# When a planner gives back a buffer of gate-output sums, and which addition the last quad's third product stands behind

## The chip, the cores and the metric

The kernel runs on one core of one Trainium2 chip. The metric is the device time of one execution in microseconds (us); lower is better. Before the change it is 394.08 us, the median of three runs (394.03 to 394.35).

## The reference

Multi-head attention feeds a two-layer network with a SiLU between the layers. Shapes: batch 8, 12 heads, 448 tokens, head size 64; so 3584 tokens of width 768, and an inner width of 2048.

```python
scores = scale * np.matmul(q, k.transpose(0, 1, 3, 2))
attn = softmax(scores)                       # over the keys
x = np.matmul(attn, v).transpose(0, 2, 1, 3).reshape(3584, 768)
h = x @ w_in                                 # 768 -> 2048
g = h * (1.0 / (1.0 + np.exp(-h)))           # SiLU
out = g @ w_out                              # 2048 -> 768, float32
```

## The kernel before, in words

**Units of attention.** A unit is one batch with four of its heads (the first batch's units are cut in two pieces of tokens). For each unit TensorE makes scores into PSUM (tiles `s`, line 345), ScalarE takes the exponential (`E`, line 382), VectorE adds two or three of the exponentials for the row sums (`T`, line 393), TensorE makes the sums and then the two products with V (tiles `a`, lines 408 and 424; "part 1" and "part 2" of a unit), and VectorE normalizes each part into `xT` (`norm`, line 479). Keys and queries come in by DMA (`rk`, `rq`) and are transposed by VectorE (`KT`, line 314; `rq`, line 332). Units mostly go in pairs; the pair spoken of here is 11 and 12, followed by units 13, 14 and so on.

**First layer.** `ffn1` (tiles `h`) multiplies `xT` with `w_in`; ScalarE's tanh (line 517) and VectorE's `gate` (line 552) make the gate outputs `G` (some of them stand in `X`). The last two batches are done as a pair of tokens' blocks with tiles `f`, lines 626 to 681.

**Second layer.** The tokens are cut into 28 tiles of 128, and two tiles make a quad: quads 0 to 13. Quad 0 is done plainly (tiles `o`). Each other quad is a two by two by two block product done with seven products of eight matmuls instead of eight products (Strassen's way, in Winograd's form). The products are called 1, 5, 6, 2, 7, 3, 4, in the order in which they are queued, and lie in PSUM tiles `p`. Products 1, 6, 7 and 4 all accumulate into the bank of product 1, the long bank, and between them each state of it is read out: after 1 and 6 and 4 by a ScalarE copy (`take_copy`, line 767), after 7 by a VectorE addition (`take_sum`, line 773). Product 3 accumulates into the bank of product 5, product 2 has its own. An addition or a copy writes an output tile `ost`, and `store` sends it out.

**The gate-output sums.** Products 5, 6 and 3 take a sum of gate outputs as their stationary operand. VectorE makes it in two halves (`combine_g`, line 696, 128x512 each): sum 5 from `G` alone (`S<-G`), sum 6 from sum 5 (`S<-S,G`, or `S<-S,X`), sum 3 from sum 6 (`S<-G,S` or `S<-X,S`). Product 7 takes a difference that is written over `G` (`G<-G`). The sums live in three buffers, tag `S`, `NSG` = 3. So sum 5 is read by product 5 and by the two halves of sum 6; sum 6 by product 6 and by the two halves of sum 3; sum 3 by product 3 alone.

**What sets the order.** The order on every engine is drawn before the program is built, by a planner (`Order`) that walks through time with a cost for each step: when an engine is free in it, it picks the next step whose inputs are ready. The steps are then issued in that order, and each engine works through its own list in order. Buffers that rotate are counted by rings: a sum is planned only when `sg_ring` has a free place,

```python
while todo and (todo[0] == 7 or sg_ring.can(1, od.now)):
    m = todo.pop(0)
    if m != 7:
        sg_ring.take()
```

and a place is given back at the end of the product that reads the sum (`op.then = sg_ring.give`, line 1199). The ring is the planner's count only. Which of the three buffers a sum gets, and the semaphores that hold its writer back until all readers of the former contents are done, come from the tile pool when the program is built.

**Waits between products.** In `queue(m)` of a quad, `first` names the read-outs that product m stands behind: those in `hard` must be done in the planner's time, the others need only have been placed already (`(took.get(x), 9.0)`). For m = 3 `first` is (5, 6, 7), of which 5 is hard. TensorE's array is used in three ways: by rows of 32 (scores), by columns of 32 (attention products, 32 small matmuls where a whole one takes 8), and whole. `times` with `strips` makes a layer's product by columns where the planner's state is "cols", so that the array isn't switched; the lists show such a product as x32 or x24 and a whole one as x8 or x6.

Of the kernel before, what the change touches and what calls it, by code (L numbers as in the profile page):

```python
# [25 lines left out]
def mm(n):  # L26
    return n / 2400.0 + 0.0026


def act(n):  # L30
    return n * 0.00087 + 0.13
# [138 lines left out]
def kernel(  # L170
# [11 lines left out]
    B, NH, S, D = q.shape  # L182
# [14 lines left out]
    NT = 2 * S // 128  # L197
# [14 lines left out]
    NE, NX3, NT_ = 9, 6, 2  # L212
    NXT = 3 * NX3
    NSG, NOST = 3, 7
    attn_scale = 1.0 / (D**0.5)

    const = ctx.enter_context(tc.tile_pool(name="const", bufs=1))
# [467 lines left out]
    def combine_g(qd, m, f0, f1):  # L685
        a, b = 2 * qd, 2 * qd + 1
        if m != 7 and (qd, m) not in S_t:
            S_t[(qd, m)] = sb.tile([128, HF, 128], FP16, name=f"S_{qd}_{m}", tag="S", bufs=NSG)
        x, y, op = {
            5: (rows(b, 0), rows(b, 1), ALU.add),  # L690
            6: (S_t.get((qd, 5)), rows(a, 0), ALU.subtract),
            7: (rows(a, 0), rows(b, 0), ALU.subtract),
            3: (rows(a, 1), S_t.get((qd, 6)), ALU.subtract),
        }[m]
        dst = rows(b, 0) if m == 7 else S_t[(qd, m)]
        nc.vector.tensor_tensor(out=dst[:, f0:f1], in0=x[:, f0:f1], in1=y[:, f0:f1], op=op)  # L696
# [3 lines left out]
    def product(qd, m, strips):  # L700
        w = {1: rows(2 * qd, 0), 2: rows(2 * qd, 1), 4: rows(2 * qd + 1, 1), 7: rows(2 * qd + 1, 0)}
        w = w[m] if m in w else S_t[(qd, m)]
        if BANK[m] == m:
            pr_t[(qd, m)] = ps.tile([128, 512], FP32, name=f"p_{qd}_{m}", tag="m", bufs=4)
        for f in range(HF):
            times(
                pr_t[(qd, BANK[m])][:, 0:OH],
                w[:, f, :],
                W_[m][:, f, :],
                f == 0 and BANK[m] == m,  # L710
                f == HF - 1,
                strips,
            )
# [174 lines left out]
    sg_ring, ost_ring = Ring(NSG), Ring(NOST)  # L888
# [240 lines left out]
    def batches(qd):  # L1129
        return {  # L1130
            (128 * t + c) // S for t in (2 * qd, 2 * qd + 1) for c in (0, 127)
        }

    def plan_sums():

        if not quads:
            return
        qd, todo = quads[0]
        if len(todo) == 4:
            gates = {}  # L1140
            for b in batches(qd):
                for f in range(NFF):
                    if len(g_op.get((b, f), ())) < (len(PIECES) if b == 0 else 1):
                        return
                    gates.setdefault(f, []).extend(g_op[(b, f)])
            gates_of[qd] = gates
        gates = gates_of[qd]
# [4 lines that stand above are left out]
            sg_op[(qd, m)] = []  # L1152
            for f0 in (0, 4):
                deps = [x for f in range(f0, f0 + 4) for x in gates[f] + gates[f + HF]]
                if m != 5:
                    deps += sg_op[(qd, {6: 5, 7: 5, 3: 6}[m])]
                sg_op[(qd, m)].append(
                    od.add(
                        Op(
                            "DVE",  # L1160
                            0.34,
                            lambda m=m, f0=f0: combine_g(qd, m, f0, f0 + 4),
                            deps,
                            0,
                        )
                    )
                )
        if not todo:
            quads.pop(0)

    def queue_quad(qd):
        quads.append((qd, [5, 6, 7, 3]))
        took = {}
        home = far_ring if qd in FAR else ost_ring

        def read(m, deps):
            def then(at):
                if m in (2, 3, 4):
                    m_ring.give(at)
                if m in (2, 3, 4, 7):  # L1180
                    home.give(at + STORE)

            fn, eng = (take_copy, "ACT") if m in OUT else (take_sum, "DVE")
            busy = act(OH) if eng == "ACT" else OH / 960.0 + 0.13
            bias = -2 if eng == "ACT" else -4
            took[m] = od.add(Op(eng, busy, lambda: fn(qd, m), deps, bias, then=then))

        def queue(m):
            first = {6: (1,), 2: (1,), 7: (6, 5), 3: (5, 6, 7), 4: (7,)}.get(m, ())

            def run():
                strips = od.mode == "cols" and bool(qk_seq or av_seq)
                op = Op("PE", HF * mm(OH), lambda: product(qd, m, strips), tail=PE_OUT)
                if BANK[m] == m:
                    m_ring.take()
                for ring, need in rings:
                    ring.take(need)
                if m in (5, 6, 3):
                    op.then = sg_ring.give
                od.on_pe(op, "cols" if strips else "full")  # L1200
                pr_op[(qd, m)] = op
                read(m, [op] + [took[x] for x in {2: (1,), 7: (5,), 3: (6,)}.get(m, ())])

            def deps():
                made = list(w_op.get(m, [None]))
                hard = {6: (1,), 7: (6,), 3: (5,), 4: (7,)}.get(m, ())
                made += [took.get(x) if x in hard else (took.get(x), 9.0) for x in first]
                if m in (1, 2, 4):
                    t = 2 * qd + m // 4
                    i = int(m != 1)  # L1210
                    for b in {(128 * t + c) // S for c in (0, 127)}:
                        for f in range(HF):
                            x = g_op.get((b, f + HF * i), [None])
                            made += [(y, f * mm(OH)) for y in x]
                    return made + ld_wout
                x = sg_op.get((qd, m), [None, None])
                return made + [x[0], (x[1], 4 * mm(OH))]

            rings = ((home, 1),) if m in OUT else ()
            moe.append((deps, 1 if BANK[m] == m else 0, run, rings))  # L1220


        for m in (1, 5, 6, 2, 7, 3, 4):
            queue(m)
# [238 lines left out]
    while True:  # L1463
        plan_turns(qk_seq[0][0][0] + 3 if qk_seq else NU)
        plan_adds()
        plan_pair()
        plan_silu()
        plan_sums()
        soon = od.step()
        if od.free["PE"] <= od.now:  # L1470
# [78 lines left out]
```

## Time and profile before

| what | value |
|---|---|
| median of three runs | 394.08 us (394.03 to 394.35) |
| the profiled execution's own time | 394.92 us |
| its span, first to last instruction | 393.1 us |
| granted TensorE clock | 1.000 |
| TensorE matmul busy | 384.6 us (98%) |
| VectorE busy | 274.4 us (70%) |
| ScalarE busy | 253.9 us (65%) |
| GpSimd busy | 89.0 us (23%) |

The profile names engines PE (TensorE matmul), PEld (its weight loads), DVE (VectorE), ACT (ScalarE), POOL (GpSimd) and SP (SyncE). A row of the timeline has the start in us from the first instruction, the time that it covers, the engine, the line of the kernel, the operation, the tile written and those read, and how many instructions of that kind follow each other; in square brackets stands how long the engine sat idle before it, and what ended that. The end of a matmul is modelled and lies after the point where the next can start, so the time that TensorE takes for a group is read from its start to the start of the next group. Buffer numbers are left out of the tiles' names: `S` is any of the sums, `xT` any of the normalized tiles.

### The profile page before, as it was taken

Reading aid. Unit: us, or ns where it says so; the run is one execution under the profiler, and the core shown is the slowest. Engines: PE = TensorE matmul, PEld = TensorE weight load, DVE = VectorE, ACT = ScalarE, POOL = GpSimd, SP = SyncE. Lnnn points to the kernel's source line nnn. Section 1 sums busy time; section 2 is a strip of 40 time slices with the busy share of each in tenths; the row PEclk is TensorE's granted clock in tenths of the full one; section 3 lists DMA queues with packets and bytes.
Section 4 is the critical chain, followed back from the end, with each engine's and each line's share of the span. In section 5 each row is a group of like instructions: output and inputs, shape, how many; then the busy total and the mean of one; then the engine's idle time right before and its main releaser. Section 6 shows DMA issues by size and latency. Waiting matters only on the chain.

```text
span 393.1 us, 10622 instructions
## 1 busy us (share of the span) xinstructions
PE 384.6 (98%) x4345; PEld 206.3 (52%) x4345; DVE 274.4 (70%) x570; ACT 253.9 (65%) x399; POOL 89.0 (23%) x173
## 2 busy tenths in 40 slices
PE   7999999999998999999999999999999999999995
PEld 6657774444454444545445444544445555556663
DVE  2466676999977787868678758665969984447441
ACT  4977885797765779766683766567793338882220
POOL 7533365515006252400643005000000000000000
PEclk9999999999999999999999999999999999999999
DMA  8999999929039482905767229102100131001333
GB/s 120 196 202 210 158 147 195 193 43 138 4 55 144 107 117 37 133 21 106 125 92 89 56 64 158 24 0 52 33 2 2 37 96 30 2 1 43 91 93 99
DMA packets 35361, 34.52 MB, mean 88 GB/s; under 512 B 11376, under 2 KB 33776, under 8 KB 35312
## 3 DMA queue, kind: packets, MB, share of 16 engines
q0 software_dynamic: 24784, 22.82, 39.7%
q1 hardware_dynamic: 9952, 10.33, 9.8%
q8 instruction: 34, 0.56, 0.6%
q10 hardware_dynamic: 576, 0.69, 0.5%
q14 instruction: 15, 0.12, 0.1%
HBM read 45.61 MB, written 11.01 MB: 144 GB/s over the span
## 4 chain that ended last, share of the span: by engine, by line
PE 95%; DVE 1%; DMA 1%; ACT 1%; issue 1%; DVEq 0%; POOLq 0%
PE p L491 30%; PE h L491 29%; PE s L345 12%; PE a L408 11%; PE f L491 8%; PE o L491 3%; PE a L424 2%; DMA rk<-in_k_dram 1%; PE z L1458 1%; ACT E L382 1%; DVE KT L314 0%; DVE S L696 0%; DVE rq L332 0%; DVE xT L479 0%; ACT ost L767 0%
## 5 line engine op out<-in xcount | busy, mean ns | idle before, releaser
L382 ACT ACTIVATE E<-s 128x896 f16<-128x896 f32 (+1 forms) x172 | 149.9, 915 | 38.6 <-PE s L345 37.1
L491 PE MATMUL h<-xT,w_in_t 128*32 128x448 f16 (+2 forms) x1086 | 117.1, 336 | 0.0
L491 PEld LDWEIGHTS <-w_in_t 128*128 128x128 f16 (+1 forms) x1158 | 71.1, 97 | 56.4 <-issue 11.5
L517 ACT ACTIVATE th<-h 128x448 f16<-128x448 f32 (+1 forms) x112 | 54.2, 494 | 36.7 <-PE h L491 31.9
L552 DVE SCALAR_TENSOR_TENSOR G<-th,h 128x448 f16<-128x448 f16 (+2 forms) x112 | 55.7, 509 | 23.4 <-ACT th L517 21.8
L767 ACT COPY ost<-p 128x384 f32<-128x384 f32 x52 | 24.9, 480 | 55.2 <-PE p L491 53.6
L491 PEld LDWEIGHTS <-G 128*128 128x128 f16 (+1 forms) x580 | 43.3, 98 | 32.7 <-issue 4.9
L345 PE MATMUL s<-rq,KT 32*128 32x448 f16 (+4 forms) x768 | 50.9, 337 | 1.0 <-DVE rq L332 0.5
L279 POOL DMA_DIRECT2D V<-in_v_dram x88 | 48.3, 558 | 13.3 <-DMA w_out_t<-in_moe_w_out_dram 6.0
L491 PE MATMUL p<-w_out_t,G 128*128 128x384 f16 (+1 forms) x328 | 49.5, 326 | 0.0
L408 PE MATMUL a<-E,V 128*32 128x448 f16 (+2 forms) x864 | 42.5, 333 | 1.3 <-DVE xT L479 1.0
L491 PEld LDWEIGHTS <-S 128*128 128x128 f16 (+1 forms) x384 | 29.8, 98 | 23.1 <-issue 2.7
L260 POOL DMA_DIRECT2D rq<-in_q_dram x27 | 15.1, 558 | 104.6 <-PE s L345 79.2
L491 PE MATMUL p<-D,S 128*128 128x384 f16 (+1 forms) x232 | 37.1, 326 | 0.0
L479 DVE SCALAR_TENSOR_TENSOR xT<-a,rdn 128x448 f16<-128x448 f32 (+1 forms) x54 | 30.4, 568 | 6.4 <-PE a L408 4.5
L345 PEld LDWEIGHTS <-KT 32*128 32x128 f16 (+2 forms) x864 | 17.5, 98 | 29.4 <-issue 27.6
L773 DVE TENSOR_TENSOR ost<-p,ost 128x384 f32<-128x384 f32 x39 | 21.6, 553 | 16.1 <-PE p L491 12.6
L408 PEld LDWEIGHTS <-V 128*32 128x32 f16 (+1 forms) x864 | 20.8, 96 | 20.1 <-issue 8.8
L393 DVE TENSOR_TENSOR T<-E,E 128x1792 f16<-128x1792 f16 x20 | 21.6, 1081 | 8.0 <-ACT E L382 8.0
L393 DVE TENSOR_TENSOR T<-T,E 128x1792 f16<-128x1792 f16 x20 | 21.6, 1082 | 5.7 <-ACT E L382 5.7
L314 DVE STREAM_TRANSPOSE KT<-rk 128x256 f32<-128x256 f32 (+3 forms) x48 | 16.6, 384 | 6.6 <-DMA rk<-in_k_dram 6.1
L491 PE MATMUL p<-D,G 128*32 128x384 f16 (+1 forms) x176 | 19.1, 326 | 0.4 <-DVE ost L773 0.4
(67 smaller groups left out, 320.4 us busy)
## 6 DMA issues: line engine op xcount, KB each, us to landing
out_dram<-ost SPq DMA_DIRECT2D x194, 48.0 KB, 1.6
rk<-in_k_dram POOLq DMA_DIRECT2D x24, 224.0 KB, 5.6
rq<-in_q_dram POOLq DMA_DIRECT2D x21, 224.0 KB, 5.6
w_in_t<-in_moe_w_in_dram POOLq DMA_DIRECT2D x6, 512.0 KB, 12.7
w_out_t<-in_moe_w_out_dram POOLq DMA_DIRECT2D x4, 768.0 KB, 13.5
V<-in_v_dram POOLq DMA_DIRECT2D x43, 64.0 KB, 3.7
V<-in_v_dram POOLq DMA_DIRECT2D x40, 48.0 KB, 3.8
out_dram<-ost SPq DMA_DIRECT2D x8, 96.0 KB, 2.1
```

The lines of the kernel that those rows point to most:

```text
L279: nc.gpsimd.dma_start(out=VT[b][32 * x : 32 * (x + 1), hs, 0:count, :], in_=v[b, hs].rearrange("h (i g) d -> i h g d", g=TPP)[:, :, first ...
L314: nc.vector.transpose(out=pairs[:, x:y, 0:count], in_=t[:, first : first + count * (y - x)].rearrange("p (x c) i -> p x c i", c=count),)
L345: nc.tensor.matmul(out=pS[p0 : p0 + 32 * (x1 - x0), h % 2, at : at + nq], lhsT=KT[(b, hg)][32 * h : 32 * (h + 1), c, x0:x1, :, e], rhs=QT[ ...
L382: nc.scalar.activation(out=E[(n, w)][0:kr, 2 * y : 2 * y + 2, 0:nk], in_=pS_t[(n, w, y)][0:kr, :, 0:nk], func=AF.Exp, scale=attn_scale,)
L393: nc.vector.tensor_tensor(out=T[n], in0=T[n] if step else E[(n, 0)], in1=E[(n, step + 1)], op=ALU.add,)
L408: nc.tensor.matmul(out=a[32 * h : 32 * (h + 1), 0:nq], lhsT=w, rhs=e[k0:k1, h, at : at + nq], start=start, stop=stop,)
L479: nc.vector.scalar_tensor_tensor(out=x3(b, cc)[:, cc % 3, 32 * g0 : 32 * g1], in0=acc[(n, part)][:, 0:nq], scalar=0.5, in1=rdn_t[n].rearra ...
L491: nc.tensor.matmul(out=out[i : i + cut], lhsT=w[:, i : i + cut], rhs=x, start=start, stop=stop, skip_group_check=True,)
L517: nc.scalar.activation(out=th, in_=h_t[(b, f, t0)][:, 0 : t1 - t0], func=AF.Tanh)
L552: nc.vector.scalar_tensor_tensor(out=dst[:, f, at + lo : at + hi], in0=th_t[(b, f, t0)][:, lo - t0 : hi - t0], scalar=1.0, in1=h_t[(b, f, ...
L767: nc.scalar.copy(out=ost(qd, *OUT[m]), in_=bank(qd, BANK[m]))
L773: nc.vector.tensor_tensor(out=t, in0=bank(qd, BANK[m]), in1=t, op=ALU.add)
```

## The change

The planner's ring now gets a buffer back only when all its readers have been placed: the place of sum 5 at the latest end among product 5 and the two halves of sum 6, that of sum 6 at the latest end among product 6 and the two halves of sum 3, that of sum 3 at the end of product 3. And in quad 13, the last, product 3 no longer needs the addition after product 7 to have been placed ahead of it.

```diff
+    LAST = NT * B // 4 - 1
...
+    sum_reads = {}
+
+    def sum_read(qd, m, at):
+        made = sum_reads.setdefault((qd, m), [])
+        made.append(at)
+        if m and len(made) == (1 if m == 3 else 3):
+            sg_ring.give(max(made))
+
     def plan_sums():
...
                             lambda m=m, f0=f0: combine_g(qd, m, f0, f0 + 4),
                             deps,
                             0,
+                            then=lambda at, m=m: sum_read(qd, {6: 5, 3: 6}.get(m), at),
...
-            first = {6: (1,), 2: (1,), 7: (6, 5), 3: (5, 6, 7), 4: (7,)}.get(m, ())
+            first = {6: (1,), 2: (1,), 7: (6, 5), 3: (5, 6) if qd == LAST else (5, 6, 7), 4: (7,)}.get(m, ())
...
                 if m in (5, 6, 3):
-                    op.then = sg_ring.give
+                    op.then = lambda at: sum_read(qd, m, at)
```

No instruction's work is changed by it, only the order that the planner draws. Where both programs are laid side by side, engine by engine, the lists of GpSimd and SyncE are the same, and ScalarE's order is the same; VectorE's list differs in three places, TensorE's in one:

- Quads 1 and 2, VectorE. Before: the difference for product 7 of quad 2 (two halves), the addition after product 7 of quad 1, sum 3 of quad 2 (two halves), the normalization of unit 11 part 2, transpose of `rq` 14, first `T` of unit 13, the addition after product 3 of quad 1, normalization of unit 12 part 1, transpose of `KT`, second `T` of unit 13, normalization of unit 12 part 2, transpose of `rq` 15. After: the addition after product 7 of quad 1, the difference for product 7 of quad 2, transpose of `rq` 14, first `T` of unit 13, the normalization of unit 11 part 2, sum 3 of quad 2, the addition after product 3 of quad 1, transposes of `KT` and `rq` 15, normalization of unit 12 part 1, second `T` of unit 13, normalization of unit 12 part 2. (A little earlier the second half of sum 6 and half of the difference of quad 1 change places with sum 5 of quad 2.)
- The same place, TensorE. Before: product 3 of quad 1 (columns), scores of unit 13, part 1 of unit 12, product 4 of quad 1 (columns), part 2 of unit 12, scores of unit 14, products 5 and 2 of quad 2 (whole), scores of unit 14. After: product 3 of quad 1 (columns), scores of unit 13, product 4 of quad 1 (whole), part 1 of unit 12, scores of unit 14, part 2 of unit 12, products 5 and 2 of quad 2 (columns), scores of unit 14.
- Quads 3 and 4, VectorE. Before: sum 6 of quad 4, the difference for product 7 of quad 4, sum 3 of quad 3, `KT`, `rq` 19, the addition after product 7 of quad 3. After: sum 3 of quad 3, `KT`, sum 6 of quad 4, the difference for product 7 of quad 4, `rq` 19, the addition after product 7 of quad 3. (The second half of sum 6 of quad 3 also goes ahead of sum 5 of quad 4.)
- Quads 8 and 9, VectorE. The tile `sx` for the last two batches (line 600) goes ahead of sum 6 of quad 9, and the addition after product 7 of quad 8 goes between the two halves of the difference for product 7 of quad 9, ahead of sum 3 of quad 9.

In quad 13 no engine's list differs.

## The prediction

> **What bounds the kernel now.** I read the page first, part 4, the chain that ended last:
>
> ```profile
> PE 95%; DVE 1%; DMA 1%; ACT 1%; issue 1%; DVEq 0%; POOLq 0%
> ```
>
> TensorE's work is nearly the whole chain, so the end moves by what TensorE gains or loses and by little else. The change removes no matmul work; it can only take away or add time in which TensorE stands still. So the second view is TensorE's own waits from 100 us on, ahead of every place where the two orders differ:
>
> ```profile
> engine line waited for: us in total, times, longest us
> PE a L408 <- DVE xT L479: 1.0, 1, 1.0
> PE p L491 <- DVE ost L773: 0.4, 1, 0.4
> ```
>
> These are all: two waits, both for VectorE, in the last three quarters of the span. After them the chain in order of time shows nothing but TensorE's groups, and ends with the last quads' products in one unbroken piece:
>
> ```profile
> 353.75 35.12 PE p L491 x216
> ```
>
> 216 matmuls in 35.12 us is 0.163 us each, which is also what one costs inside a group below. There is no hole in the tail.
>
> **The first wait, quads 1 and 2.** TensorE's rows, then VectorE's and two of ScalarE's, from the timeline:
>
> ```profile
> 117.16 1.47 PE L491 MATMUL p<-w_out_t,S 128*32 128x384 f16 x32
> 118.56 0.58 PE L345 MATMUL s<-rq,KT 32*128 32x448 f16 x8
> 120.13 0.94 PE L408 MATMUL a<-E,V 128*32 128x448 f16 x16 [0.99 <-DVE xT L479]
> 120.88 1.49 PE L491 MATMUL p<-D,G 128*32 128x384 f16 x32
> 122.18 0.94 PE L408 MATMUL a<-E,V 128*32 128x448 f16 x16
> 123.06 0.57 PE L345 MATMUL s<-rq,KT 32*128 32x448 f16 x8
> 123.56 1.47 PE L491 MATMUL p<-D,S 128*128 128x384 f16 x8
> 124.87 1.46 PE L491 MATMUL p<-w_out_t,G 128*128 128x384 f16 x8
> 126.27 0.57 PE L345 MATMUL s<-rq,KT 32*128 32x448 f16 x8
> ```
> ```profile
> 115.19 0.74 DVE L696 TENSOR_TENSOR G<-G 128x512 f16<-128x512 f16 x2
> 115.85 0.55 DVE L773 TENSOR_TENSOR ost<-p,ost 128x384 f32<-128x384 f32 x1
> 118.68 0.76 DVE L696 TENSOR_TENSOR S<-G,S 128x512 f16<-128x512 f16 x2 [2.28 <-PE p L491]
> 119.36 0.62 DVE L479 SCALAR_TENSOR_TENSOR xT<-a,rdn 128x448 f16<-128x448 f32 x1
> 119.90 0.63 DVE L332 STREAM_TRANSPOSE rq<-rq 128x448 f32<-128x448 f32 x1
> 120.45 1.05 DVE L393 TENSOR_TENSOR T<-E,E 128x1792 f16<-128x1792 f16 x1
> ...
> 122.42 0.69 DVE L314 STREAM_TRANSPOSE KT<-rk 128x256 f32<-128x256 f32 x2
> ```
> ```profile
> 115.08 1.73 ACT L382 ACTIVATE E<-s 128x896 f16<-128x896 f32 x2 [1.52 <-PE s L345]
> ...
> 119.17 1.73 ACT L382 ACTIVATE E<-s 128x896 f16<-128x896 f32 x2 [1.99 <-PE s L345]
> ```
>
> The reader is to see one chain of blame. VectorE reaches sum 3 of quad 2 (`S<-G,S`) and stands 2.28 us, because the buffer that this sum gets still holds sum 3 of quad 1, which product 3 (TensorE's 117.16) is reading; it is let go 0.06 us after the scores that follow that product have begun (118.68 against 118.56). Behind the blocked sum, in the same list, is the normalization of unit 11 part 2 (119.36), and TensorE's part 1 of unit 12 wants the PSUM bank that it empties: 0.99 us of standing.
>
> After: the normalization is ahead of the sum. I put VectorE's new order end to end from 115.19, with these durations whole (a pessimistic sum, since neighbours overlap a little): addition 0.55, difference 0.74, `rq` 0.63, `T` 1.05, normalization 0.62, which ends at 118.78. `T` starts at 117.11 and wants the exponentials that end at 115.08 + 1.73 = 116.81. TensorE's new order from 118.56, each step from start to start of the rows above: scores 0.50 (123.06 to 123.56), whole product 4 before another use of the array 1.40 (124.87 to 126.27), part 1 then 0.88 to scores (122.18 to 123.06), scores 0.50, part 2 then 0.75 (120.13 to 120.88), product 5 by columns 1.30 (120.88 to 122.18), product 2 by columns before scores 1.40 (117.16 to 118.56). That is 6.73 us, against 126.27 - 118.56 = 7.71 before: **0.98 us gained**. It holds 0.09 us for one more switch of the array than before (1.40 against 1.31, 123.56 to 124.87). The two products that go to columns and the one that leaves them cost nothing: 1.30 against 1.31.
>
> Is anything late in the new order? Part 1 of unit 12 starts at 120.46, 1.7 us behind the normalization's 118.78. The next scores at 121.34 want `rq` 14 (117.11) and the exponentials that end at 119.17 + 1.73 = 120.90. Part 2 at 121.84 wants the addition after product 3 of quad 1: sum 3 of quad 2 (0.76) and the addition (0.55) end at 118.78 + 1.31 = 120.09. Product 5 of quad 2 at 122.59 wants ScalarE's copy of product 4, which comes right behind the exponentials. Product 2 at 123.89 wants the normalization of part 1: `KT` 0.69 and `rq` 0.63 end at 121.41, part 1's end is at about 121.4, so 122.03. Sum 3 of quad 2 still waits for product 3, but nothing that TensorE needs soon stands behind it.
>
> A rule that speaks against this step: the Trainium skill, "TensorEngine Tiling (Array Packing)", Key Properties, says that changing the tiling mode drains the array. By it the extra switch would cost up to the tail of a group, 1.46 as modelled against 1.31, so 0.15 instead of 0.09 us, and the sum below would be 0.06 us smaller; the trace has the next group's start ahead of that tail's end (126.27 against 124.87 + 1.46), so I go by the rows.
>
> **The second wait, quads 3 and 4.**
>
> ```profile
> 170.71 0.58 PE L345 MATMUL s<-rq,KT 32*128 32x448 f16 x8
> 171.21 1.47 PE L491 MATMUL p<-w_out_t,G 128*128 128x384 f16 x8
> 172.53 1.46 PE L491 MATMUL p<-D,S 128*128 128x384 f16 x8
> 173.92 0.57 PE L345 MATMUL s<-rq,KT 32*128 32x448 f16 x8
> 174.51 1.47 PE L491 MATMUL p<-w_out_t,S 128*128 128x384 f16 x8
> 176.43 1.46 PE L491 MATMUL p<-D,G 128*128 128x384 f16 x8 [0.44 <-DVE ost L773]
> 177.81 0.41 PE L345 MATMUL s<-rq,KT 32*64 32x448 f16 x8
> ```
> ```profile
> 169.42 0.75 DVE L696 TENSOR_TENSOR S<-S,G 128x512 f16<-128x512 f16 x2
> 170.09 0.75 DVE L696 TENSOR_TENSOR G<-G 128x512 f16<-128x512 f16 x2
> 174.03 0.76 DVE L696 TENSOR_TENSOR S<-X,S 128x512 f16<-128x512 f16 x2 [3.18 <-PE p L491]
> ...
> 175.85 0.52 DVE L773 TENSOR_TENSOR ost<-p,ost 128x384 f32<-128x384 f32 x1
> ```
>
> The same thing: sum 3 of quad 3 was given the buffer of sum 5 of quad 4, which product 5 of quad 4 (172.53) reads, and VectorE stands 3.18 us. Product 3 of quad 3 wants that sum and starts 0.59 us after the scores instead of 0.50; product 4 wants the addition after product 7, which is queued behind the sum, `KT` and `rq`, and starts 1.92 us after product 3 instead of 1.32 (171.21 to 172.53).
>
> After: sum 3 of quad 3 stands first and gets the buffer of sum 5 of quad 3, whose product was over before the scores of 170.71. From 169.42, end to end: sum 3 0.76, `KT` 0.69, sum 6 of quad 4 0.75, difference 0.75, `rq` 0.63, addition 0.52, which ends at 173.52. Product 4 of quad 3 would start at 173.92 + 0.50 + 1.32 = 175.74, 2.2 us behind it, and the scores 1.39 us later (172.53 to 173.92), at 177.13 instead of 177.81: **0.68 us gained**. Sum 3 of quad 4 now waits for product 5 of quad 4, but its own product comes a dozen us later.
>
> **The other moves.** In quads 8 and 9 `sx` goes ahead of sum 6 of quad 9:
>
> ```profile
> 309.80 0.76 DVE L696 TENSOR_TENSOR S<-S,G 128x512 f16<-128x512 f16 x2
> ...
> 312.29 0.85 DVE L600 TENSOR_TENSOR sx<-xT,sx 128x1344 f16<-128x1344 f16 x1
> ```
> ```profile
> 311.40 0.81 PE L491 MATMUL p<-D,S 128*128 128x384 f16 x4
> ```
>
> The sum would end at 309.80 + 0.76 + 0.85 = 311.41 at the latest, its first half 0.38 earlier, and product 6 of quad 9 starts at 311.40 with the first half only. Cost nothing to 0.1 us; I take nothing. Here the cover is thin, and each us beyond it would be TensorE's. The last quad's edit I cost at nothing: no engine's list differs there, and the tail had no hole that it could close.
>
> **The sum.** 0.98 + 0.68 = 1.66 us. Against the profiled execution, 394.92 us (span 393.1), that gives 393.26; the median of the runs is 0.84 us below the profiled one, and the orders are fixed, so the same stalls are in both: 394.08 - 1.66 = **392.4 us**.
>
> **The rivals.** *One of the two goes, the other comes back* behind something that the rows don't show (chance 0.09). First alone: 393.1; second alone: 393.4. For it: the second addition's new place has five steps ahead of it; against it: margins of 1.7 and 2.2 us.
>
> *The buffers' waits move instead of going* (0.05). The semaphores that hold a sum's writer were there before, and the planner's count only chooses the order; two of the sums still wait for products. If other readers queue behind them, the time is 394.1. Against it: the lists show who stands behind.
>
> *A late load blocks VectorE*, slower than before (0.03). The transpose of `rq` 14 is now ahead of the normalization that part 1 of unit 12 needs.
>
> ```profile
> 90.44 0.57 POOL L260 DMA_DIRECT2D rq<-in_q_dram  x1
> ...
> DMA to landing us min/median/max: 3.7/4.5/6.6
> ```
>
> From landing to normalization are 0.63 + 1.05 + 0.62 = 2.30 us. TensorE loses from a landing after 118.2 on, all is lost from 119.8 on, and at 120.8 the kernel is at 395.1. The rows say that it is issued at 90.44 and lands by 97.1.
>
> *Products by columns load their weights in the open*, also slower (0.02). One product more than before goes by columns, 32 weight loads instead of 8. If the 24 more cost 0.08 us each (half of a matmul's 0.163), 1.9 us would be lost, and the kernel be at 394.3; it decides from 0.07 us each on. The Trainium skill's page "TensorEngine Tiling (Array Packing)", Restrictions, has column tiling without fast weight load, which would make it so. The rows 120.88 to 122.18 and 123.56 to 124.87 show no such cost.
>
> **How the numbers follow.** Forecast 0.81, rivals 0.09, 0.05, 0.03, 0.02. A measurement of this kernel can tell about 0.2%, 0.79 us, from no change, so the line lies at 393.29. Faster: the forecast and two thirds of the first rival, 0.87; same: the rest of it and the second, 0.08; slower: 0.05. The range goes up to the second gain alone, 393.4, and down to 391.9: the runs' spread of 0.3, a free switch (0.09) and 0.1 for the rounding of the rows below the forecast.
>
> **What would show it.** Right: TensorE's waits from 100 us on no longer name `xT` and `ost`; VectorE's normalization of unit 11 part 2 starts near 118 instead of 119.36; the scores of 126.27 come at 125.3; from there to 166 every row is 1.0 us earlier, and behind 178 every row 1.7. Wrong: a new wait of TensorE at products 4 or 6 of any quad, a wait of VectorE for a DMA at `rq` or `KT`, or a product x32 that takes more than 1.4 to the next start.

## The result

The kernel after takes 392.77 us (median), the kernel before in the same comparison 394.14 us. The medians differ by 1.4 us. The ratio of the runs, which is not that of the medians, is 0.9957 with a 95% interval of 0.9943 to 0.9971: about 1.7 us faster, between 1.1 and 2.2. The means differ by as much, 394.33 and 392.62 us; one run of before took 395.25. One of the six executions of the kernel after, 408.34 us at a granted clock of 0.952, was in a slower state and stands outside the ratio and the means. The forecast was 392.4 us, in a range of 391.9 to 393.4.

The profiled execution took 392.49 us with a span of 390.7 us, 2.4 us shorter than the profiled one of before. That is more than the change brought, and the profile says where the rest lies. The first look is again at TensorE's waits, now over the whole of the kernel after:

```profile
engine line waited for: us in total, times, longest us
PE z L1468 <- DVE zeros L228: 1.0, 1, 1.0
PE s L346 <- ACT E L383: 0.4, 1, 0.4
PE s L346 <- DVE rq L333: 0.3, 1, 0.3
PE a L409 <- issue: 0.3, 1, 0.3
```

Asked for 100 us on, the same view is empty. The two waits that the forecast rested on are gone and none has come in their place; the four left are in the opening. Line numbers are higher by one here than in the kernel before, and by two in the first four experiments.

The place of the first wait, TensorE and then VectorE:

```profile
116.37 1.47 PE L492 MATMUL p<-w_out_t,S 128*32 128x384 f16 x32
117.78 0.57 PE L346 MATMUL s<-rq,KT 32*128 32x448 f16 x8
118.28 1.47 PE L492 MATMUL p<-D,G 128*128 128x384 f16 x8
119.69 0.94 PE L409 MATMUL a<-E,V 128*32 128x448 f16 x16
120.56 0.57 PE L346 MATMUL s<-rq,KT 32*128 32x448 f16 x8
121.07 0.94 PE L409 MATMUL a<-E,V 128*32 128x448 f16 x16
121.83 1.47 PE L492 MATMUL p<-D,S 128*32 128x384 f16 x32
123.13 1.47 PE L492 MATMUL p<-w_out_t,G 128*32 128x384 f16 x32
124.54 0.57 PE L346 MATMUL s<-rq,KT 32*128 32x448 f16 x8
```
```profile
114.41 0.54 DVE L774 TENSOR_TENSOR ost<-p,ost 128x384 f32<-128x384 f32 x1
114.87 0.73 DVE L697 TENSOR_TENSOR G<-G 128x512 f16<-128x512 f16 x2
115.53 0.64 DVE L333 STREAM_TRANSPOSE rq<-rq 128x448 f32<-128x448 f32 x1
116.09 1.06 DVE L394 TENSOR_TENSOR T<-E,E 128x1792 f16<-128x1792 f16 x1
117.07 0.62 DVE L480 SCALAR_TENSOR_TENSOR xT<-a,rdn 128x448 f16<-128x448 f32 x1
117.90 0.76 DVE L697 TENSOR_TENSOR S<-G,S 128x512 f16<-128x512 f16 x2 [0.21 <-PE p L492]
```

Between the scores of unit 13 and the second scores of unit 14 lie 124.54 - 117.78 = 6.76 us, where before it was 7.71. The sum still waits for product 3 (0.21 us instead of 2.28), at a time when the normalization (117.07) is already through. The place of the second wait:

```profile
172.19 0.57 PE L346 MATMUL s<-rq,KT 32*128 32x448 f16 x8
172.69 1.47 PE L492 MATMUL p<-w_out_t,S 128*128 128x384 f16 x8
174.00 1.46 PE L492 MATMUL p<-D,G 128*128 128x384 f16 x8
175.40 0.60 PE L346 MATMUL s<-rq,KT 32*64 32x448 f16 x16
```
```profile
167.69 0.76 DVE L697 TENSOR_TENSOR S<-X,S 128x512 f16<-128x512 f16 x2
168.35 0.70 DVE L315 STREAM_TRANSPOSE KT<-rk 128x256 f32<-128x256 f32 x2
168.98 0.72 DVE L697 TENSOR_TENSOR S<-S,G 128x512 f16<-128x512 f16 x2
169.61 0.76 DVE L697 TENSOR_TENSOR G<-G 128x512 f16<-128x512 f16 x2
170.28 0.64 DVE L333 STREAM_TRANSPOSE rq<-rq 128x448 f32<-128x448 f32 x1
171.05 0.56 DVE L774 TENSOR_TENSOR ost<-p,ost 128x384 f32<-128x384 f32 x1
171.52 1.08 DVE L394 TENSOR_TENSOR T<-E,E 128x1792 f16<-128x1792 f16 x1
172.52 0.75 DVE L697 TENSOR_TENSOR S<-G,S 128x512 f16<-128x512 f16 x2
```

From scores to scores 3.21 us instead of 3.89; VectorE goes through without standing.

0.95 and 0.68 are 1.63 us of the 2.4. The other 0.8 us of the profiled difference lies ahead of every place where the two orders differ. Product 1 of quad 1, a row with the same lists of every engine in front of it, stands at

```profile
103.39 1.46 PE L491 MATMUL p<-w_out_t,G 128*128 128x384 f16 x8
```

in the kernel before, and in the kernel after at

```profile
102.58 1.46 PE L492 MATMUL p<-w_out_t,G 128*128 128x384 f16 x8
```

So in what follows each profile is also read as its span less the start of that row. I call it the rest: 393.1 - 103.39 = 289.7 us before, 390.7 - 102.58 = 288.1 after.

### The profile page after: what moved, and what is told of

Read it like the earlier page. It is cut to its first block, busy times and chain, and to the rows that moved or that the text cites. A ratio compares the mean times of both kernels' runs of the same rounds, so it can differ in the third digit from the quotient of the medians.

```text
span 390.7 us, 10672 instructions
## 1 busy us (share of the span) xinstructions
PE 384.3 (98%) x4369; PEld 206.3 (53%) x4369; DVE 274.6 (70%) x570; ACT 253.7 (65%) x399; POOL 89.1 (23%) x173
## 4 chain that ended last, share of the span: by engine, by line
PE 97%; DMA 1%; ACT 1%; issue 0%; POOL 0%; DVE 0%; POOLq 0%
PE p L492 31%; PE h L492 29%; PE s L346 13%; PE a L409 11%; PE f L492 8%; PE o L492 3%; PE a L425 2%; DMA rq<-in_q_dram 1%; PE z L1468 1%; ACT E L383 1%; POOL rk L255 0%; ACT ost L768 0%; DVE rq L333 0%; ACT th L518 0%; POOLq L1543 0%
## 5 line engine op out<-in xcount | busy, mean ns | idle before, releaser
L492 PE MATMUL p<-w_out_t,S 128*128 128x384 f16 (+1 forms) x152 | 19.1, 326 | 0.0
```

Of the source, the lines that this page charges most:

```text
L492: nc.tensor.matmul(out=out[i : i + cut], lhsT=w[:, i : i + cut], rhs=x, start=start, stop=stop, skip_group_check=True,)
```

## The experiments

My theory: a sum for which the planner saw a free buffer got one that a product was still reading; VectorE stood at the sum, and behind it stood a normalization in one place and an addition in the other, each of which TensorE needed. Rivals: the stall only moves; the new order on TensorE is what gains; the sums wait for their inputs rather than their buffers. All times of before in this section are of the comparison in which the kernel ran. A gain in us goes by the ratio, so it can differ by a few tenths from the difference of the medians beside it; the rest is the finer measure, from one profile of each kernel.

### The held buffer at the first place alone

```diff
+    HELD = (1, 2)
...
+                            then=lambda at, m=m: qd in HELD and sum_read(qd, {6: 5, 3: 6}.get(m), at),
...
+                    op.then = (lambda at: sum_read(qd, m, at)) if qd in HELD else sg_ring.give
```

(and `LAST` = -1, so that the last quad is as before; the next three have the same lines with another `HELD`)

> The held buffer only for quads 1 and 2; every other quad gives its places back as before, and the last quad's edit is left out. Only the lists of quads 1 and 2 differ from the kernel before. Theory (two separate stalls of VectorE, each at a sum whose buffer is still read): 0.95 us faster than before, TensorE's wait for xT at part 1 of unit 12 gone, its wait for ost in quads 3 and 4 still there with about 0.4 us and the sum's idle of about 3.2 us ahead of it. Rival (the stall only moves): less than 0.3 us faster, with a new wait of TensorE between 118 and 128 us. Rival (the gain comes from elsewhere): as fast as the kernel after, 1.4 us or more.

Measured: 393.38 us against 394.19, ratio 0.9975 (0.9965 to 0.9986), that is 1.0 us faster (0.6 to 1.4). The rest is 391.1 - 102.31 = 288.8, 0.9 us less than before. From 100 us on TensorE has one wait left:

```profile
PE p L493 <- DVE ost L775: 0.4, 1, 0.4
```

The second place is as it was, seen on VectorE and on TensorE:

```profile
172.01 0.76 DVE L698 TENSOR_TENSOR S<-X,S 128x512 f16<-128x512 f16 x2 [3.18 <-PE p L493]
```
```profile
174.41 1.46 PE L493 MATMUL p<-D,G 128*128 128x384 f16 x8 [0.44 <-DVE ost L775]
```

### The held buffer at the second place alone

`HELD = (3, 4)`.

> The held buffer only for quads 3 and 4. TensorE's list is that of the kernel before; VectorE's differs only in quads 3 and 4. Theory: 0.65 to 0.7 us faster than before; TensorE's wait for ost gone, its wait for xT in quads 1 and 2 (0.99 us) still there. Rival (the stall only moves): less than 0.2 us. Rival (TensorE's switch of product 4 to whole width is what gains): no gain here.

Measured: 393.63 us against 394.19, ratio 0.9984 (0.9975 to 0.9994), 0.6 us faster (0.2 to 1.0). The rest is 392.2 - 103.12 = 289.1, 0.6 us less than before. Now the other wait is the only one left from 100 us on, and the first place is as it was:

```profile
PE a L410 <- DVE xT L481: 1.0, 1, 1.0
```

```profile
118.41 0.76 DVE L698 TENSOR_TENSOR S<-G,S 128x512 f16<-128x512 f16 x2 [2.28 <-PE p L493]
119.09 0.62 DVE L481 SCALAR_TENSOR_TENSOR xT<-a,rdn 128x448 f16<-128x448 f32 x1
```
```profile
119.86 0.94 PE L410 MATMUL a<-E,V 128*32 128x448 f16 x16 [0.99 <-DVE xT L481]
```

TensorE's list is that of before here, from end to end, so this part of the gain owes nothing to an order of TensorE's. The two parts add up to the whole change (0.9 + 0.6 against 1.6), and neither stall moved elsewhere.

### The held buffer in quads 5 to 13 alone

`HELD = tuple(range(5, 14))`.

> The held buffer only for quads 5 to 13, where the lists differ only in VectorE's order at quads 8 and 9. Theory: within 0.2 us of the kernel before, both of TensorE's waits still there, and no new one at product 6 of quad 9. Rival (the thin cover at product 6 of quad 9 is not enough): up to 0.4 us slower with a wait of TensorE for S near 311 us.

Measured: 394.1 us against 394.19, ratio 1.0001 (0.9992 to 1.0010). The rest is 393.2 - 103.54 = 289.7, that of before. Nothing is won or lost here. TensorE's waits from 100 us on are the two of before, and none is at product 6 of quad 9:

```profile
310.51 0.76 DVE L698 TENSOR_TENSOR S<-S,G 128x512 f16<-128x512 f16 x2
```
```profile
311.53 1.46 PE L493 MATMUL p<-D,S 128*128 128x384 f16 x8
```

Sum 6 of quad 9 ends at 311.27, 0.26 us ahead of its product. The prediction had it end 0.01 us behind at the latest, with whole durations laid end to end; so the cover was thin, but less thin than I had computed.

### The last quad's edit alone

`HELD = ()` and `LAST` as in the change.

> The last quad's edit alone, without the held buffer. No engine's order differs from the kernel before. Theory: the same time within 0.2 us, and the last products as one unbroken row in the trace. Rival (product 3 of the last quad did stand behind the addition): 0.1 to 0.7 us faster. It also says how far two kernels with the same orders differ from each other in this measurement.

Measured: 394.19 us against 394.19, ratio 0.9990 (0.9971 to 1.0010), which alone doesn't exclude some tenths. The profile does: the rest is 392.4 - 102.70 = 289.7, that of before to a tenth. Its span is 0.7 us shorter than that of before, all of it ahead of product 1 of quad 1.

### A fourth buffer, and the room for it

Four buffers of sums fit only if another pool gives room; so first the base, the kernel before with

```diff
-            t = sb.tile([128, OH], FP32, name=name, tag="ost", bufs=NOST)
+            t = sb.tile([128, OH], FP32, name=name, tag="ost", bufs=5)
```

> The kernel before with five real buffers for the output tiles instead of seven; the planner still counts seven, so every engine's order is that of before. It is the base for the next two, which need the room. Theory: an output tile is free again a few us after its addition, so within 0.2 us of before, and no new wait of VectorE or ScalarE for out_dram over 0.5 us. Rival: new waits of VectorE for out_dram in quads 1 to 4, and slower by as much as they hold TensorE.

Measured: 394.18 us against 394.26, ratio 0.9998 (0.9988 to 1.0007); the rest is 392.5 - 102.82 = 289.7. Five output tiles are enough. The expectation of no new wait for `out_dram` holds only in substance:

```profile
268.77 0.56 DVE L773 TENSOR_TENSOR ost<-p,ost 128x384 f32<-128x384 f32 x1 [1.31 <-DMA out_dram<-ost]
```

This row is put down to `out_dram` where that of before, at 269.35, is put down to a product; but VectorE stood 1.30 us there before too. Then, on top of it, with every engine's order still that of before:

```diff
-            S_t[(qd, m)] = sb.tile([128, HF, 128], FP16, name=f"S_{qd}_{m}", tag="S", bufs=NSG)
+            S_t[(qd, m)] = sb.tile([128, HF, 128], FP16, name=f"S_{qd}_{m}", tag="S", bufs=4)
```

> The kernel before, every engine's order as before, but four real buffers for the sums (the planner still counts three), with five output tiles. The two sums that stood idle then get a buffer that nobody reads. Theory (it is the buffer that holds the sum, and the order does harm only through it): both waits of TensorE gone, 1.7 us faster than before, that is as fast as the kernel after or up to 0.1 us faster, since the array is switched once less. Rival (the new order is itself what gains, whole product 4 ahead of part 1 of unit 12): under 0.8 us faster. Rival (the sum waits for its inputs, not its buffer): no gain, VectorE still idle 2 to 3 us ahead of sum 3.

Measured: 392.62 us against 394.26, ratio 0.9953 (0.9941 to 0.9966), 1.9 us faster (1.3 to 2.3). The rest is 390.5 - 102.53 = 288.0. VectorE at the first place, in the old order:

```profile
115.00 0.55 DVE L773 TENSOR_TENSOR ost<-p,ost 128x384 f32<-128x384 f32 x1
115.47 0.75 DVE L696 TENSOR_TENSOR S<-G,S 128x512 f16<-128x512 f16 x2
116.53 0.62 DVE L479 SCALAR_TENSOR_TENSOR xT<-a,rdn 128x448 f16<-128x448 f32 x1 [0.32 <-PE a L408]
```
```profile
117.71 0.58 PE L345 MATMUL s<-rq,KT 32*128 32x448 f16 x8
118.22 0.94 PE L408 MATMUL a<-E,V 128*32 128x448 f16 x16
```

The sum stands at the same place in the list and does not wait at all: its inputs had been there, only its buffer was taken. At the second place, too, neither the sum nor product 4 waits:

```profile
168.85 0.75 DVE L696 TENSOR_TENSOR S<-X,S 128x512 f16<-128x512 f16 x2
```
```profile
173.83 1.46 PE L491 MATMUL p<-D,G 128*128 128x384 f16 x8
```

This is the run that settles the cause. The order of before is harmless once the buffer is free; the change mends the same fault by the order instead of by memory. From these scores to the second scores of unit 14 it takes 124.36 - 117.71 = 6.65 us (the row below), 0.11 less than the kernel after, which has one more switch of the array there:

```profile
124.36 0.57 PE L345 MATMUL s<-rq,KT 32*128 32x448 f16 x8
```

### The kernel after with a fourth buffer

The same two lines in the kernel after.

> The kernel after with four real buffers for the sums and five output tiles, orders as in the kernel after. Theory: TensorE has no wait left from 100 us on in the kernel after, so nothing is to be had: within 0.2 us of the kernel after, 1.5 to 1.7 us faster than before. Rival (waits for buffers still cost in the kernel after, below what the wait rows show): 0.3 us or more faster than the kernel after.

Measured: 392.45 us against 394.26, ratio 0.9953 (0.9941 to 0.9966); the rest is 391.0 - 102.93 = 288.1, that of the kernel after. No wait for a buffer of the sums is left in it that costs anything.

### Four buffers that the planner knows of

```diff
-    NSG, NOST = 3, 7
+    NSG, NOST = 4, 7
```

on the kernel after, with five real output tiles.

> The kernel after with four buffers both in the planner's count and in fact, and five real output tiles; the planner then draws another order from quad 1 on (many differences on TensorE, VectorE and ScalarE). Theory: the time is TensorE's work with its switches, and no wait is left to remove, so within 0.3 us of the kernel after, either way; a difference then is the number of array switches times 0.09 us. Rival (a longer look ahead lets VectorE's normalizations be late again): 0.5 us or more slower than the kernel after, with a wait of TensorE for xT.

Measured: 392.27 us against 394.26, ratio 0.9949 (0.9936 to 0.9961); the rest is 390.6 - 102.69 = 287.9. TensorE has no wait from 100 us on here either. It is the lowest of all medians, but its interval covers the ratio of the kernel after; the rests put it 0.2 us ahead, from one profile each. Whether it beats the kernel after isn't settled. Counted in the traces from 100 us on, TensorE changes between its three uses 109 times in the kernel after, with or without the fourth buffer, and 108 times here, in the kernel before and in the old order with the fourth buffer. The expectation set a difference at 0.09 us a switch, so one switch less is about half of the 0.2.

## Why the prediction was right

- **The bound.** That TensorE's work is the chain and that only its two waits could go held: with both gone the profile has no wait of TensorE from 100 us on, and the two halves tried alone add up.
- **The first place, 0.98 us.** Measured 0.95 (7.71 to 6.76) in the profile after. The 0.03 us between them are hundredths in several steps: product 4 and product 2 took 1.41 us to the next start where I had used 1.40, the second scores 0.51 for 0.50, part 2 0.76 for 0.75, part 1 0.87 for 0.88. The normalization was ready 2.0 us ahead of its need (117.07 + 0.62 against 119.69) where I had computed 1.7, since I had laid the durations end to end.
- **The second place, 0.68 us.** Measured 0.68. The addition ended at 171.61, 2.4 us ahead of product 4 (174.00); I had 2.2. I had also written that sum 3 of quad 4 would now wait for product 5 of quad 4; it didn't (172.52, with no idle before it), which changes nothing in the sum.
- **The extra switch of the array, 0.09 us.** The fourth buffer with the old order gives 0.11 between the same two scores. The Trainium skill ("TensorEngine Tiling (Array Packing)", Key Properties) says that a change of tiling mode drains the TensorE; my estimate by it was up to 0.15. The measured 0.11, from one pair of profiles, lies nearer to the rows. That settles a price here and not whether the array drains.
- **Columns for products 5 and 2.** 121.83 to 123.13 is 1.30 us, what a whole product takes; the rival of weights loaded in the open falls. The Trainium skill ("TensorEngine Tiling (Array Packing)", Restrictions) has column tiling without fast weight load; no cost of that shows in the trace, where the step of 1.30 us is no longer than a whole product's 1.31 (123.56 to 124.87 in the kernel before). One of my signs of being wrong was a product x32 that takes more than 1.4 us to the next start, and product 2 took 1.41 (123.13 to 124.54). That is the step ahead of another use of the array, 1.40 in the kernel before (117.16 to 118.56); I had set the sign too near to it.
- **Edits costed at nothing.** Quads 5 to 13 and the last quad, tried alone, show the rest of before to a tenth of a us.
- **The sum, 1.66 us.** 1.63 by rows, 1.6 by the rests, 1.7 (1.1 to 2.2) by the times. The median is 0.4 us above the forecast. No term of the sum is off by that; five of the six executions of the kernel after lie between 392.18 and 392.90 us, and how much of this is the opening wasn't taken apart.
- **Not foreseen.** I had written that every row behind 178 us would be 1.7 us earlier and those from the first place to 166 us 1.0. In this pair of profiles it is 0.8 more, from the opening, of which I had not thought when I set rows of two executions beside each other.

The rival of a late load can be dismissed from the profile after: `rq` 14 is transposed at 115.53 without a wait. It wasn't tried with a later load.

## What to carry to other kernels

A planner that counts a buffer as free when its main reader is done, but not its other readers, draws an order that the semaphores then correct at run time, and an engine that works through its list in order passes that correction on to everything behind the blocked step. Look for idle time of an engine that is *not* the bound, ended by the bound, and ask what stands behind it in the list; here 5.5 us of VectorE's idle cost TensorE 1.7 (the rest is 289.7 in the kernel before and 288.0 with a free buffer), of which the change wins back 1.6. The two edits here whose lists came out the same, the last quad's and the five output tiles, cost nothing; and before the profiles of two kernels are subtracted, find the last row with equal work ahead of it and subtract from there.

## What I had not expected of the hardware

The opening varies from profile to profile by more than the change's smaller part is worth. Up to product 1 of quad 1 all these kernels have the same lists on every engine that leads to it, yet it starts between 102.31 and 103.54 us in ten profiles. In the kernel before TensorE is busy 27.22 of the first 30 us, in the kernel after 27.99:

```profile
0.00:30.00 30.00, 27.22 (x503) 19.07 (x507) 13.92 (x47) 21.76 (x25) 16.12 (x30) 1.00 1.06 173
```
```profile
0.00:30.00 30.00, 27.99 (x522) 19.95 (x523) 14.45 (x49) 22.38 (x25) 16.67 (x31) 1.00 1.06 176
```

(the first is of before, the second of after; the columns are the stretch and its length, then busy us and instructions of PE, PEld, DVE, ACT and POOL, the granted clock, and the share and rate of the DMA engines). TensorE's listed waits ahead of 100 us come to 2.7 us before and 2.0 after, so most of the 0.8 lies in them. The share of the DMA engines is 1.06 in that stretch in both, so it may be the loads' arrival that varies; that wasn't tried and stays open. Each kernel was profiled once, so no profile shows it for two executions of one kernel; but the kernel before, two experiments with exactly its lists and one whose lists differ only at quads 8 and 9 start that row at 102.70 to 103.54. From that row to the end, kernels with the same orders agree to 0.1 us: 289.7 in four of them.
